# Three of six loads of keys go through ScalarE's DMA queue, in a kernel of windowed attention and two dense blocks

## The chip, the cores and the metric

One NeuronCore of one Trainium2 chip runs the whole kernel. Its engines are TensorE (PE; PEld is its weight load), VectorE (DVE), ScalarE (ACT), GpSimd (POOL) and SyncE (SP). Each has an instruction queue of its own, and they wait for one another through semaphores. The metric is the device time of one execution in microseconds (us), the median of several runs.

## The reference

The attention scores each query against the keys within 16 positions and against 24 block summaries of the keys (the maximum over 32 positions); the values are extended by block means. Its output goes through two dense blocks.

```python
k_sum = k.reshape(B, H, nb, block, D).max(axis=3)      # B, H, S, D = 2, 8, 768, 64; block = 32
v_sum = v.reshape(B, H, nb, block, D).mean(axis=3)
scores_l = scale * np.matmul(q, k.transpose(0, 1, 3, 2))
mask_l = np.abs(pos[:, None] - pos[None, :]) < window  # window = 16
scores_s = scale * np.einsum('bhsd,bhnd->bhsn', q, k_sum) + np.log(block)
...
a = softmax(concatenate([where(mask_l, scores_l, -1e9), scores_s]))
x = matmul(a, concatenate([v, v_sum], axis=2))         # then 1536 tokens x 512
...
h = np.maximum(x @ w_in, 0.0);  x = h * h @ w_out      # first block, 512 -> 2048 -> 512
h = x @ w_in;  g = P(h) / Q(h);  out = g @ w_out       # second block, P and Q polynomials
```

## The kernel before

The kernel runs the attention first, in pieces, and lays the first steps of the dense blocks between them; from about 125 us on, it is the two dense blocks alone: for each of 16 blocks of 128 hidden features and each of three groups of 512 tokens, `l1` (line 630, h) and `l2` (line 724, y) with three matmuls where full precision needs the product of a high and a low part. The weights come as 64-bit words and are decoded on ScalarE, VectorE and GpSimd.

The order of the work of the first part is written out by hand in the string `ORDER`: a list of names that is walked once, and each name calls a function that puts instructions into the queues of its engines. An engine runs its instructions in the order in which they were put there. The names that matter here:

- `E0` to `E5` are `e_load(j)`: load slot j of the keys of the first batch, 128 x 512 floats, 256 KB. Two slots share a buffer: slots 0 and 1 are `early_105`, 2 and 3 `early_106`, 4 and 5 `early_107`. All six go through SyncE's queue (`nc.sync`, line 316), in the order 0, 1, 2, 4, then a load of v (`v1`, line 335), then 3, 5.
- `t0` to `t3` are `k_tr(p)` (line 403): PE transposes the keys of head pair p into two PSUM banks `pk`. t0 reads slots 0 and 1, t1 slots 1 and 2, t2 slots 3 and 4, t3 slots 4 and 5.
- `l0`, `k0`, `l1`, `k1` ... are `k_lin` (line 424): a copy out of one of these banks into `kt`, on ScalarE (on VectorE with a star).
- `q_0`, `q_1`, `Q1` load queries (line 361) through SyncE: four loads of 128 KB, then two of 256 KB.
- `X0`, `X1`, ... are `keep_busy` (line 290): filler matmuls on PE, whose result nobody reads.

The table of ScalarE's functions is loaded by `preload_act_table_set` (line 778), which stands ahead of the walk through the list, so it is ScalarE's first instruction.

Each load reports its landing on one of eight lanes, named DMAHW0 to DMAHW7 in the program. The builder deals the lanes in turn over all queues; a load on a lane that an earlier load had waits, in the queue of the engine that issues it, until that earlier load has landed.

Of the kernel before, what the change touches and what calls it, by code (L numbers as in the profile page):

```python
# [17 lines left out]

ORDER = (
# [32 lines left out]
def tile_window_attention_moe_moe(  # L52
# [13 lines left out]
    nc = tc.nc  # L66
# [111 lines left out]
    T6 = 6  # L178
    NS = 3
    bt = ap.tile([P, WT + (T6 // 2 + 2 * NS) * NB], F32, name="b6", bufs=1)  # L180
    b6 = [bt[:, r * NB:r * NB + HK] for r in range(T6 // 2)]
    b8 = [bt[:, (T6 // 2 + i) * NB:(T6 // 2 + i) * NB + HK] for i in range(2 * NS)]
# [105 lines left out]
    def keep_busy(i):  # L288
# [3 lines left out]
    consts = dict(  # L292
        _i0=c_idle,
        _id=lambda: make_identity(nc, ident), _pr=c_more,
        _m0=lambda: nc.vector.memset(wide, 0.0), _m1=c_window,
        _ml=lambda: nc.vector.memset(mk[:, :, WT:], math.log(BLK) * SC), _m2=c_masks, _b8=c_blocks, _bw=c_blocks6,
    )
# [11 lines left out]
    def flat(src, h, lo, n):  # L309

        x = src[h:h + 4].rearrange("h (p r) d -> (h p) (r d)", r=TR)
        return x[lo * P:(lo + n) * P].rearrange("(s p) x -> p s x", p=P)

    def e_load(j):

        nc.sync.dma_start(
            out=k8[j].rearrange("p (s x) -> p s x", s=1), in_=flat(k[0], j // NS * 4, j % NS, 1)
        )

# [285 lines left out]
    N0 = [0, 5, NF, NF + 9]  # L605
# [167 lines left out]
    G1 = len(tok1) * FS[0] - LEAD[0]  # L773
    dve, act = nc.vector.tensor_copy, nc.scalar.copy
    some, rest = slice(0, 4), slice(4, NWIN)
    v0 = [early[4 + p][:, 0:2 * T6 * D].rearrange("p (h r d) -> p h r d", r=T6, d=D) for p in range(NP)]

    nc.scalar.preload_act_table_set("natural_log_exp_and_others")
    nc.gpsimd.memset(abc[:, 4:5], (1.0 + 1e-6) * 2.0 ** -62)
    nc.gpsimd.memset(abc[:, 5:6], -62.0 * math.log(2.0))  # L780

    def w_next(j, *a):
# [4 lines left out]
    vec = lambda c: nc.vector if c else nc.gpsimd  # L787
    parts = dict(
        E=e_load, v=lambda p: s_load(0, 2 * p, v0[p]), Q=q_load,
        N=lambda i: v_load(i // 4, i % 4 // 2, i % 2), J=k_load,  # L790
        Z=z_load, I=lambda i: w_next(3),
# [12 lines left out]
    G2 = len(tok1) * FS[0] + len(tok2) * FS[1]  # L804
# [122 lines left out]
```

## Time and profile before

| | us |
|---|---|
| median of 3 runs | 601.13 (600.59 to 602.09) |
| profiled execution | 601.2 |
| its span, first to last instruction | 599.5 |

Engines, over the span: PE 592.1 us busy, ACT 392.1, DVE 384.0, POOL 311.6. The chain of work that ended last lies to 93% on PE. The share of PE is so high that the interesting part is the little that is missing from it: nearly all of it lies in the first 100 us. A chain of waits is read backward from the last instruction: each step names what released the next one, a load by "DMA", an engine's queue by a "q" behind its name.

### The profile page before, as it was taken

The page shows a single profiled execution, that of the slowest core. Times are in us where ns is not written, and L with a number is a line of the kernel's source. Part 1 is how long each engine was busy: PE and PEld are TensorE (multiplying, and loading weights), DVE is VectorE, ACT ScalarE, POOL GpSimd, SP SyncE. Part 2 cuts the span into 40 slices and gives each one's busy share as a digit, 9 for nine tenths or more (in the row PEclk, how much of TensorE's full clock was granted, in tenths as well). Part 3 has the DMA queues.
Part 4 walks back from the last instruction along what each step waited for, and adds up shares of the span by engine and source line. Part 5 has one row for each costly group of instructions (what it writes and reads, how often), then busy time and mean ns, then how long its engine had stood idle before and what let it go on. Part 6 is the DMA issues. An engine that isn't in the chain of part 4 may idle for free.

```text
span 599.5 us, 9779 instructions
## 1 busy us (share of the span) xinstructions
PE 592.1 (99%) x3560; PEld 493.6 (82%) x3560; DVE 384.0 (64%) x801; ACT 392.1 (65%) x704; POOL 311.6 (52%) x316
## 2 busy tenths in 40 slices
PE   8999999999999999999999999999999999999997
PEld 8988788888888888888888888888888888888885
DVE  5999977666723331112374778998777876686765
ACT  4999777555644442222565789988888887777772
POOL 1776545412554462222776488676655665445542
PEclk9999999999999999999999999999999999999999
DMA  8989974344532220000254103121211200010101
GB/s 231 248 170 238 243 163 125 102 141 141 175 107 84 93 69 1 0 1 0 71 174 143 35 1 105 36 72 36 71 35 36 71 2 0 1 70 2 47 25 70
DMA packets 64576, 51.49 MB, mean 86 GB/s; under 512 B 39824, under 2 KB 57488, under 8 KB 64528
## 3 DMA queue, kind: packets, MB, share of 16 engines
q1 hardware_dynamic: 64384, 50.74, 30.5%
q8 instruction: 28, 0.46, 0.3%
q14 instruction: 20, 0.16, 0.1%
q10 hardware_dynamic: 144, 0.13, 0.1%
HBM read 47.71 MB, written 3.15 MB: 85 GB/s over the span
## 4 chain that ended last, share of the span: by engine, by line
PE 93%; DVE 3%; DMA 2%; ACT 1%; SPq 0%; issue 0%; DVEq 0%; ACTq 0%
PE h L630 44%; PE y L724 42%; PE pav L577 2%; PE pss L507 2%; PE ptp L557 1%; DMA early<-in_k_dram 1%; PE pt L485 1%; DMA early<-in_v_dram 1%; PE pk L403 1%; PE spare L290 1%; PE pvs L450 0%; DVE pr L523 0%; PE pk L412 0%; DVE acc L756 0%; DVE mx L540 0%; DVE wl L167 0%
## 5 line engine op out<-in xcount | busy, mean ns | idle before, releaser
L630 PE MATMUL h<-xh,wh 128*128 128x512 f32 x384 | 150.6, 392 | 0.0
L630 PE MATMUL h<-xh,wl 128*128 128x512 f32 x384 | 149.5, 389 | 0.0
L630 PE MATMUL h<-xl,wh 128*128 128x512 f32 x384 | 149.5, 389 | 0.0
L654 POOL TENSOR_TENSOR q<-q,u 128x512 f32<-128x512 f32 x48 | 65.2, 1358 | 96.3 <-ACT q L651 91.6
L700 POOL TENSOR_TENSOR sl<-r,sh 128x512 fp32r<-128x512 f32 x42 | 55.0, 1310 | 97.6 <-PE y L724 80.5
L645 DVE TENSOR_TENSOR r<-r,h 128x512 f32<-128x512 f32 x48 | 32.9, 686 | 111.7 <-ACT r L640 104.1
L167 POOL TENSOR_TENSOR wl<-wdec,wh 128x512 fp32r<-128x512 f32 x52 | 69.1, 1334 | 49.6 <-ACT wh L162 35.9
L630 PEld LDWEIGHTS h<-xh,wl 128*128 128x128 f32 x384 | 72.0, 188 | 15.1
L630 PEld LDWEIGHTS h<-xh,wh 128*128 128x128 f32 x384 | 72.1, 188 | 14.7
L630 PEld LDWEIGHTS h<-xl,wh 128*128 128x128 f32 x384 | 72.1, 188 | 14.5
L724 PE MATMUL y<-sh,wh 128*128 128x512 f32 x192 | 75.3, 392 | 0.0
L724 PE MATMUL y<-wh,sl 128*128 128x512 f32 x192 | 74.8, 390 | 0.1
L724 PE MATMUL y<-sl,wh 128*128 128x512 f32 x192 | 74.8, 390 | 0.0
L724 PE MATMUL y<-sh,wl 128*128 128x512 f32 x192 | 74.7, 389 | 0.0
L724 PE MATMUL y<-wh,sh 128*128 128x512 f32 x192 | 74.7, 389 | 0.0
L724 PE MATMUL y<-wl,sh 128*128 128x512 f32 x192 | 74.7, 389 | 0.0
L640 ACT ACTIVATE r<-h 128x512 f32<-128x512 f32 x48 | 28.6, 596 | 66.7 <-PE y L724 35.0
L700 POOL TENSOR_TENSOR sl<-p,sh 128x512 fp32r<-128x512 f32 x48 | 63.1, 1315 | 8.5 <-ACT sh L693 7.1
L676 DVE SCALAR_TENSOR_TENSOR q<-q,h 128x512 f32<-128x512 f32 x48 | 32.9, 686 | 41.6 <-ACT h L672 41.6
L162 ACT CAST wh<-wdec 128x512 fp32r<-128x512 f32 x64 | 39.6, 621 | 27.3 <-DVE wdec L151 27.3
L151 DVE SCALAR_TENSOR_TENSOR wdec<-wraw,wdec 128x512 int32<-128x512 int32 x64 | 49.8, 778 | 2.2
L142 ACT ACTIVATE wdec<-wraw 128x512 f32<-128x512 f32 x64 | 42.3, 666 | 10.6 <-POOL wl L167 6.0
(92 smaller groups left out, 1021.3 us busy)
## 6 DMA issues: line engine op xcount, KB each, us to landing
wraw<-in_moe_w_in_dram SPq DMA_DIRECT2D x32, 512.0 KB, 3.8
wraw<-in_moe_w_out_dram SPq DMA_DIRECT2D x32, 512.0 KB, 3.4
early<-in_v_dram SPq DMA_DIRECT2D x40, 96.0 KB, 4.2
out_dram<-acc SPq DMA_DIRECT2D x11, 256.0 KB, 2.1
acc<-in_q_dram SPq DMA_DIRECT2D x10, 256.0 KB, 6.2
early<-in_k_dram SPq DMA_DIRECT2D x6, 256.0 KB, 5.0
early<-in_v_dram SPq DMA_DIRECT2D x4, 384.0 KB, 5.5
kst<-in_k_dram SPq DMA_DIRECT2D x8, 192.0 KB, 5.4
```

Of the source, the lines that this page charges most:

```text
L142: nc.scalar.activation(out=f32(t), in_=f32(r[:, :, 1]), func=AF.Prelu, scale=2.0 ** -112, alpha=-(2.0 ** 32))
L151: nc.vector.scalar_tensor_tensor(out=t, in0=low, scalar=29, in1=t, op0=ALU.logical_shift_right, op1=ALU.bitwise_or)
L162: copy(out=wt[n][0][:, j], in_=f32(wdec[n, j]))
L167: eng.tensor_tensor(out=tl[:, j], in0=t, in1=f32(th[:, j]), op=ALU.subtract)
L507: nc.tensor.matmul(psc[u][e][w * LO:(w + 1) * LO, c * HK:(c + 1) * HK], lhsT=qz[u % 2][r, c * P + w * LO:c * P + (w + 1) * LO], rhs=kt[2 * ...
L630: nc.tensor.matmul(hq[g][:, 0:n], lhsT=w[:, 0, ws], rhs=x[:, part, ts], start=(part == 0 and j == 0), stop=(part == KC - 1 and j == 2),)
L640: nc.scalar.activation(out=r, in_=hq[g][:, 0:n], func=AF.Relu)
L645: nc.vector.tensor_tensor(out=eq[g], in0=eq[g], in1=hq.pop(g)[:, 0:n], op=ALU.mult)
L654: nc.gpsimd.tensor_tensor(out=q_, in0=q_, in1=u_, op=ALU.mult)
L676: nc.vector.scalar_tensor_tensor(out=q_, in0=q_, scalar=1.0 + 1e-6, in1=z_, op0=ALU.add, op1=ALU.mult)
L700: eng.tensor_tensor(out=sl[:, 0:n], in0=eq.pop(g), in1=f32(sh[:, 0:n]), op=ALU.subtract)
L724: nc.tensor.matmul(o, lhsT=lt, rhs=rt, start=(f == 0 and j == 0 and d * m % 512 == 0), stop=(f == FS[ps] - 1 and j == 2 and (d + 1) * m % ...
```

## The change

`e_load` issues slots 1, 3 and 4 through ScalarE's queue (`nc.scalar`) and slots 0, 2 and 5 through SyncE's. The preload of the table of functions leaves its place ahead of the list and becomes an entry of it, `_pl`, right behind `E3`. Otherwise the list holds the same names in the same order (its lines are broken elsewhere).

```diff
 ORDER = (
     "K1 _i0 _m0 E0 K2 X31 X32 X33 X34 X35 X0 X1 E1 K0 _id t0 k0* l0 c0 B0* E2 _ml _m1 E4 _m2 t1 "
-    "_pr v1 K3 E3 t2 k1 l2 k2 l1* c1 E5 t3 l3 q_0 k3 B1* c2 q_1 q0 z0 X2 c3 S1 q1 z1 B3 X3 s0 s1 "
+    "_pr v1 K3 E3 _pl t2 k1 l2 k2 l1* c1 E5 t3 l3 q_0 k3 B1* c2 q_1 q0 z0 X2 c3 S1 q1 z1 B3 X3 "
...
         _id=lambda: make_identity(nc, ident), _pr=c_more,
+        _pl=lambda: nc.scalar.preload_act_table_set("natural_log_exp_and_others"),
...
     def e_load(j):
 
-        nc.sync.dma_start(
+        dma = nc.scalar if j in (1, 3, 4) else nc.sync
+        dma.dma_start(
             out=k8[j].rearrange("p (s x) -> p s x", s=1), in_=flat(k[0], j // NS * 4, j % NS, 1)
         )
...
-    nc.scalar.preload_act_table_set("natural_log_exp_and_others")
     nc.gpsimd.memset(abc[:, 4:5], (1.0 + 1e-6) * 2.0 ** -62)
```

ScalarE's queue at the program's start, before (kt0 to kt3 are the four pairs of keys, pk the PSUM banks of the transposes):

```order
L922 UNCONDITIONAL_BRANCH [waits barrier_Pool_Activation_PE_DVE_SP_release]
L778 ACT_TABLE_LOAD
L424 COPY kt0_98<-pk_143 128x12x12x4 [waits DVE_49,PE_49]
L424 COPY kt1_99<-pk_124 128x12x12x4 [waits PE_49]
L424 COPY kt2_100<-pk_131 128x12x12x4 [waits PE_49]
L424 COPY kt2_100<-pk_132 128x12x12x4 [waits PE_49]
```

The same place in the change:

```order
L923 UNCONDITIONAL_BRANCH [waits barrier_Pool_Activation_PE_DVE_SP_release]
L318 DMA early_105<-in_k_dram 128x512
L426 ACT_TABLE_LOAD [waits DVE_49]
L426 COPY kt0_98<-pk_142 128x12x12x4 [waits PE_49]
L318 DMA early_107<-in_k_dram 128x512 [waits DMAHW5_49]
L318 DMA early_106<-in_k_dram 128x512 [waits DMAHW7_49]
L295 ACT_TABLE_LOAD
L426 COPY kt1_99<-pk_123 128x12x12x4 [waits PE_49]
```

Slot 1 stands first; slots 4 (`early_107`) and 3 (`early_106`) stand behind the first copy, each with a wait for a lane; a table load stands ahead of that copy and another behind slot 3.

SyncE's queue at the program's start, before (acc is the buffer of the queries):

```order
L316 DMA early_105<-in_k_dram 128x512 x2
L316 DMA early_106<-in_k_dram 128x512
L316 DMA early_107<-in_k_dram 128x512
L335 DMA early_110<-in_v_dram 128x2x384
L316 DMA early_106<-in_k_dram 128x512
L316 DMA early_107<-in_k_dram 128x512
L361 DMA acc_80<-in_q_dram 128x4x64
L361 DMA acc_80<-in_q_dram 128x4x64 [waits DMAHW0_49]
L361 DMA acc_80<-in_q_dram 128x4x64 [waits DMAHW1_49]
```

The same place in the change:

```order
L318 DMA early_105<-in_k_dram 128x512
L318 DMA early_106<-in_k_dram 128x512
L337 DMA early_110<-in_v_dram 128x2x384
L318 DMA early_107<-in_k_dram 128x512
L363 DMA acc_80<-in_q_dram 128x4x64 x3
L363 DMA acc_80<-in_q_dram 128x4x64 [waits DMAHW0_49]
L363 DMA acc_80<-in_q_dram 128x8x64 [waits DMAHW1_49]
L363 DMA acc_80<-in_q_dram 128x8x64 [waits DMAHW2_49]
L129 DMA wraw_395<-in_moe_w_in_dram 128x4x256 [waits DMAHW3_49]
```

SyncE's first eight loads were four slots, v, two slots and one q; its first seven that wait for no lane are now two slots, v, one slot and three q. The order of PE's instructions is the same in both; t2's first matmul waits for lane 7 in the change (lane 5 before).

## Rows read from the trace of the kernel before

**Rows 1.** The page, part 1: busy time, share of the span, instructions

```profile
PE 592.1 (99%) x3560; PEld 493.6 (82%) x3560; DVE 384.0 (64%) x801; ACT 392.1 (65%) x704; POOL 311.6 (52%) x316
```

**Rows 2.** Busy time by stage: stretch, length, PE, PEld, DVE, ACT, POOL, clock, DMA

```profile
0.00:100.00 100.00, 96.64 (x1292) 84.17 (x1294) 82.02 (x332) 78.72 (x192) 57.24 (x116) 1.00 0.89 206
...
200.00:300.00 100.00, 100.00 (x442) 82.79 (x442) 23.64 (x39) 32.55 (x56) 39.17 (x31) 1.00 0.09 29
```

**Rows 3.** The waits of PE: us in total, times, longest

```profile
PE spare L290 <- DVE pp L285: 1.2, 1, 1.2
PE pav L577 <- DMA early<-in_v_dram: 0.8, 1, 0.8
PE pk L403 <- DMA early<-in_k_dram: 0.6, 1, 0.6
PE ptp L557 <- DVE mx L523: 0.6, 1, 0.6
```

**Rows 4.** The chain of waits from the start: start us, us, what

```profile
1.71 0.43 SPq L316
...
2.18 0.43 SPq L316
...
2.65 0.43 SPq L335
...
3.13 5.96 DMA early<-in_k_dram
...
9.14 3.86 PE pk L403 x77
```

**Rows 5.** DMA issues, us to landing: slots 0, 1, 2, 4, v, third q

```profile
early<-in_k_dram SPq DMA_DIRECT2D x1, 256.0 KB, 2.7
...
early<-in_k_dram SPq DMA_DIRECT2D x1, 256.0 KB, 2.9
...
early<-in_k_dram SPq DMA_DIRECT2D x1, 256.0 KB, 4.7
...
early<-in_k_dram SPq DMA_DIRECT2D x1, 256.0 KB, 5.2
...
early<-in_v_dram SPq DMA_DIRECT2D x1, 384.0 KB, 5.7
...
acc<-in_q_dram SPq DMA_DIRECT2D x1, 128.0 KB, 5.6
```

**Rows 6.** Timeline of SyncE's queue, the third load of q: start us, us

```profile
5.72 0.61 SPq L361 DMA_DIRECT2D acc<-in_q_dram  x1
```

**Rows 7.** Timeline of ScalarE from the start: start us, us, what

```profile
0.80 1.28 ACT L778 ACT_TABLE_LOAD   x1 [0.80 <-PEq L909]
5.70 0.64 ACT L424 COPY kt<-pk 128x576 f32<-128x576 f32 x1 [3.62 <-PE pk L403]
```

**Rows 8.** Timeline of PE: fillers, t0 with t1, t2 with t3, later fillers

```profile
1.23 3.36 PE L290 MATMUL spare<-pp 120*128 120x128 f32 x14 [1.23 <-DVE pp L285]
4.51 4.01 PE L403 MATMUL pk<-ident,early 128*64 128x96 f32 x96
9.14 3.86 PE L403 MATMUL pk<-ident,early 128*64 128x96 f32 x96 [0.61 <-DMA early<-in_k_dram]
...
16.20 2.50 PE L290 MATMUL spare<-pp 120*128 120x128 f32 x20
```

**Rows 9.** Stretches at the end; the clock is the number behind POOL's

```profile
597.00:598.00 1.00, 0.00 (x0) 0.00 (x0) 0.00 (x0) 0.00 (x0) 0.00 (x0) 1.00 1.00 347
...
598.60:599.40 0.80, 0.00 (x0) 0.00 (x0) 0.00 (x0) 0.00 (x0) 0.00 (x0) 0.50 0.00 0
```

**Rows 10.** Timeline of PE at the end: its last matmul

```profile
595.29 0.39 PE L724 MATMUL y<-wh,sl 128*128 128x512 f32 x1
```

42 rows, old and new, of the table ORDER are left out of this document.

## Prediction

> **What bounds the kernel now.** I read the page's engine list first [rows 1]: TensorE (PE) is busy 592.1 of 599.5 us, the next engine 392.1. Then the table by stage [rows 2]: in the first 100 us PE is busy 96.64, from 200 to 300 us 100.00. So nothing that happens after the first stage can be hidden by slack on PE, because there is none; and what PE loses in the first stage is added to the end one for one, unless one of its few waits there shrinks by as much. All of PE's idle time with a known releaser is four waits [rows 3]: 1.2 us at the start, 0.6 us before the transposes of keys (pk L403), 0.8 us for v, 0.6 us for VectorE. The program's order on PE is fixed, and the filler matmuls (spare L290) are instructions of that order like all others: a late PE runs them all, so they absorb no delay.
>
> The change touches the second of these waits. The chain of waits [rows 4] shows it: SyncE issues the loads of the key slots one after another, 0.47 us apart; slot 3 is issued at 3.13 us, lands 5.96 us later, and PE starts the transposes t2 at 9.14 us. PE had run out of work at 8.52 us (4.51 + 4.01 [rows 8]).
>
> **What the change removes.** Three issues leave SyncE's queue, so all that stands behind them there moves up by up to 3 x 0.47 = 1.4 us. If all three went out at once on ScalarE, slot 3 would be issued near 1.7 us instead of 3.13. What could that give? The landings say that the transfers, not the issues, set the pace: slot 4 lands at 2.18 + 5.2 = 7.4, v at 2.65 + 5.7 = 8.35, slot 3 at 9.09 [rows 4, 5], 0.7 to 1.0 us apart though issued 0.47 apart. And PE could win no more than the 0.6 us of its wait, as its work lasts to 8.52 us. The Trainium skill says the same (DMA: Bandwidth & Descriptors, section Issuing engines are not separate DMA queues): loads issued on several engines share the same 16 DMA engines, and only the sequencer's issue time is saved. By that rule alone the sum would be 0 to -0.6 us; by the order of instructions below it is not that small.
>
> **What the change moves, and into what.** ScalarE's queue is in order, and the list of work puts l0, the copy of the first transposed keys, ahead of slots 4 and 3. In the order of ScalarE's instructions after the change, slot 1 goes out first; then a table load and the first copy kt<-pk, which waits for PE; then slot 4, which waits for lane 5; then slot 3, which waits for lane 7; then a second table load. So two of the three loads are not issued at the start at all. The copy ran at 5.70 us and took 0.64 [rows 7]: slot 3 cannot be issued before about 6.3 + 0.4 = 6.7 us, against 3.13 before.
>
> The lanes cost more. Lanes are dealt by the time at which the builder expects a load to go out: slots 1, 0, 2 have lanes 0, 1, 2, v 3, slot 5 lane 4, and SyncE's next three loads, of q, take 5, 6 and 7 (they are the three that wait for nothing, and the fourth q waits for lane 0). So slot 4 waits until the first q has landed, slot 3 until the third q has. When is that? Before, the third q was issued at 5.72 us and landed 5.6 us later, at 11.3 [rows 5, 6]. Behind the change slots 4 and 3 are no longer ahead of it. Their shares are what their landings add: slot 4 (2.18 + 5.2) - (1.71 + 4.7) = 0.97 us, slot 3 9.09 - 8.35 = 0.74. That leaves 11.3 - 1.7 = 9.6 us. Bounds: 7.0 us, if q moves up by its issue time (5.72 - 1.4 = 4.3) and then flies as quickly as slot 0 (2.7); 11.3, if nothing is gained.
>
> From 9.6 us slot 3 needs its own flight. The trace shows 2.7 us for slot 0 on empty engines, 2.9 for slot 1 with one load ahead, and 5.96 for slot 3 itself behind five others in one ring. It now has a ring of its own with only slot 4 just ahead, so I take 3.0, near slot 1's 2.9; the ends are 2.7 and 6.0. With 0.1 us for the issue that lies between, slot 3 lands, and t2 starts, at **12.7 us** instead of 9.14: **+3.6 us**. On the bounds it is 9.7 to 17.3, so +0.6 to +8.2.
>
> **What else is moved.** (a) The table load, 1.28 us [rows 7], is now two, since the first copy comes ahead of the preload. The first runs behind slot 1's issue and is over near 2.6 us, three before PE has anything to copy; the second and the copy of t1 (0.64 us) start when slot 3 is issued and end 1.9 us later, under slot 3's flight of 2.7 or more. Zero; with that cover gone it would be 1.28. (b) Slots 0 and 1 start together, not 0.45 us apart. t0 needs both, but waits behind 14 fillers until 4.5 us [rows 8]; zero, within 0.3 either way. (c) Slot 2 moves up by one issue; t1 starts near 6.5 us, about its landing at 1.71 + 4.7 = 6.4; zero to -0.2. (d) v, slot 5 and q land earlier. Nobody on the path waits for them there.
>
> **The clock.** PE now has nothing to do from 8.52 to about 12.7 us, 4.2 us; before, its longest stop was 1.2 us. Two places tell what such a stop does. At the end the last matmul ends at 595.7 us [rows 10]; the granted clock is still 1.00 at 597 to 598 us and 0.50, the level of 1.2 GHz, at 598.6 [rows 9]: it had fallen within 2.9 us of idling. At the start, the 14 fillers take 3.36 us, 0.24 each, while 20 of the same kind take 2.50 later, 0.125 each [rows 8]: PE ran at half speed for its first 3.3 us of work. So a stop of 4.2 us, if it does what the end shows, costs half of 3.3 us behind it: **+1.6 us**; 0 if the clock holds, 3.3 if it stays low twice as long.
>
> **What is late next.** Everything of the attention hangs on t2 and t3 through PE, so ScalarE, VectorE and GpSimd move along with it. The two waits left, 0.8 us for v and 0.6 for VectorE [rows 3], could shrink, as weights and later loads that don't depend on PE come relatively earlier. The v load is itself issued after a PE step; I take **-0.4 us**, bounds 0 and -1.4.
>
> Sum on the profiled execution: 601.2 + 3.6 + 1.6 - 0.4 = 606.0 us. That execution is 0.07 above the median of the three runs (601.13), so against the median 605.9.
>
> **The rivals.**
> *The same wait, but the clock holds.* The stop is 4.2 us, not much more than the 2.9 us after which it had fallen at the end, and one fall is thin evidence. Time: 601.13 + 3.6 - 0.4 = 604.3.
> *Not slower: the lanes are free early.* The place is slot 3's issue on ScalarE. If the third q lands near the lower bound of 7.0 us, slot 3 goes out then and lands near 9.9: +0.7 us and no stop long enough for the clock, 601.8. The point from which it decides: with a flight of 3.0, the result leaves the band of no change only if slot 3 is issued after about 8.3 us. For it: the engines carry 768 KB less ahead of that q in SyncE's ring. Against it: 512 KB of that is merely unsent, and all landings before show 0.7 to 1.0 us for each 256 KB.
> *The loads do go out first*, as the words of the change have it: if ScalarE issued all three ahead of its copies, slot 3 would land by about 8.4 and PE's 0.6 us would go: 600.5. The order of instructions speaks against it flatly.
> *Slot 3 stands behind SyncE's traffic.* If its flight is 6.0 us as before, with q and the first weights ahead of it, t2 starts at 15.7: +6.6 + 1.6 - 0.4, 608.9. The Trainium skill (DMA: Bandwidth & Descriptors, section Queues, rings and completion order) says that each DMA engine takes turns between the rings that have work, a packet at a time, which speaks against a full 6.0. No row here shows two loaded rings at once; by that rule the flight is nearer the short end, and the sum the likeliest one above.
>
> **How the numbers follow.** Likeliest, wait and fallen clock, 605.9: 0.50, with a range of its own of 603.9 to 608.2 from a landing one to two us off. Wait alone, 604.3: 0.27. Slot 3 behind the traffic, 608.9: 0.10. Lanes free early, 601.8: 0.08. Loads first, 600.5: 0.03. The rest, 0.02, I leave to what I don't see, half of it faster. The range of 602.6 to 608.8 leaves out the two small cases below and most of the one above. About 0.3%, 1.8 us, is what a measurement of this kernel can tell from no change, so slower begins at 602.9. The first three cases, less a tail of the second, give slower 0.85; the two at 601.8 and 600.5 and that tail give same 0.13; faster 0.02, since PE's whole idle time at this spot is 0.6 us.
>
> **What would show it.** In the profile after: slot 1 issued on ScalarE near 0.8 us, but slots 4 and 3 only after the first copy, each at the moment the first and third q land, near 8.7 and 9.6; two table loads; PE idle before the second group of pk transposes for about 4 us, released by the load of k; fillers or transposes behind it at half speed and a granted clock under 1.00 near 11 to 16 us; after 100 us the same PE work as before, shifted. I am wrong if slot 3 is issued before 8.3 us, if the second group starts before 11 us, or if a later wait of PE takes the delay back.

## The result, and the profile after

The changed kernel takes 610.73 us (median of 4 runs, 607.68 to 611.14), the kernel before 601.61 in the same comparison (600.59 to 602.14): 1.0143 times as long, 95% interval 1.0106 to 1.0179. It is slower, as forecast, but by 9.1 us between the medians where 4.8 were forecast, and above the range. The profiled execution took 610.62 us, its span 608.9 against 599.5 before: +9.4 us. These 9.4 us are what has to be found.

The page's first part and the stages come first, as in [rows 1, 2]; columns are stretch, length, PE, PEld, DVE, ACT, POOL, clock, share of the DMA engines, GB/s:

```profile
PE 595.4 (98%) x3560; PEld 496.8 (82%) x3560; DVE 383.4 (63%) x801; ACT 393.4 (65%) x705; POOL 312.1 (51%) x316
```

```profile
12.00:16.00 4.00, 0.00 (x0) 0.00 (x0) 1.33 (x3) 0.27 (x1) 0.00 (x0) 0.78 1.12 291
16.00:20.00 4.00, 3.38 (x50) 3.38 (x51) 0.00 (x0) 0.64 (x1) 0.00 (x0) 0.50 0.47 117
...
0.00:100.00 100.00, 90.66 (x1190) 79.63 (x1190) 74.18 (x305) 72.80 (x176) 50.47 (x102) 0.97 0.82 196
200.00:300.00 100.00, 100.00 (x443) 82.84 (x442) 22.77 (x38) 31.48 (x55) 37.94 (x30) 1.00 0.08 27
```

PE does nothing at all from 12 to 16 us, and works at the lower of its two clock levels (0.50, 1.2 GHz) from 16 to 20. The stage from 200 to 300 us is full, as before: the loss lies at the start and is never made up.

The waits of PE, to be held against [rows 3] (us in total, times, longest):

```profile
PE pk L405 <- DMA early<-in_k_dram: 6.9, 1, 6.9
PE spare L290 <- DVE pp L285: 1.2, 1, 1.2
PE ptp L559 <- DVE mx L525: 0.6, 1, 0.6
PE pav L579 <- DMA early<-in_v_dram: 0.6, 1, 0.6
```

The four waits are the same four. Together they grew from 3.2 to 9.3 us, by 6.1. PE's busy time grew by 3.3 (592.1 to 595.4): together the 9.4. The timeline of PE, as in [rows 8], shows the two halves (start us, us, what, idle before and releaser):

```profile
1.23 3.36 PE L290 MATMUL spare<-pp 120*128 120x128 f32 x14 [1.23 <-DVE pp L285]
4.52 5.17 PE L405 MATMUL pk<-ident,early 128*64 128x96 f32 x96
16.62 5.86 PE L405 MATMUL pk<-ident,early 128*64 128x96 f32 x96 [6.94 <-DMA early<-in_k_dram]
22.41 0.66 PE L487 MATMUL pt<-ident,acc 128*128 128x128 f32 x4
```

t2 starts at 16.62 us, not at 9.14: +7.48. t2 and t3 take 5.86 us, not 3.86, and the transposes of q behind them start at 22.41, not at 12.93: +9.48, so +2.0 for the lower clock. Nearly the whole difference of the spans is there by 22.4 us; all that comes later gives back 0.1. (t0 and t1 took 5.17 instead of 4.01. PE's rate rose later in this run: 34 of its matmuls run from 5 to 7 us, as many as from 8 to 9 alone, where the kernel before has 32 from 5 to 6. The clock column reads 1.00 there in both kernels, but the trace's first entry for the clock stands at 7.44 us, and at 4.55 before. The delay lies under the wait for slot 3 and costs nothing.)

Why t2 is late stands in the chain of waits, as in [rows 4], and in ScalarE's timeline, as in [rows 7]:

```profile
3.74 6.21 DMA acc<-in_q_dram
...
9.97 6.61 DMA early<-in_k_dram
...
16.62 5.86 PE pk L405 x80
```

```profile
0.80 0.41 ACTq L318 DMA_DIRECT2D early<-in_k_dram  x1
1.48 1.28 ACT L426 ACT_TABLE_LOAD   x1 [1.48 <-DVE pk L393]
6.53 0.64 ACT L426 COPY kt<-pk 128x576 f32<-128x576 f32 x1 [3.77 <-PE pk L405]
8.88 1.43 ACTq L318 DMA_DIRECT2D early<-in_k_dram  x2
10.34 1.28 ACT L295 ACT_TABLE_LOAD   x1 [3.17 <-DMA acc<-in_q_dram]
```

Slot 1 goes out at 0.80 us. Then comes the copy at 6.53; behind it slot 4 goes out at 8.88, when the first load of q lands (8.86), and slot 3 at 9.97, when the third has (9.95). The order of steps is the predicted one, instruction by instruction. What was not predicted is the 6.61 us that slot 3 takes from there.

### The profile page after: what moved, and what is told of

Read it like the earlier page. It is cut to its first block, busy times and chain, and to the rows that moved or that the text cites. A ratio compares the mean times of both kernels' runs of the same rounds, so it can differ in the third digit from the quotient of the medians.

```text
span 608.9 us, 9778 instructions
## 1 busy us (share of the span) xinstructions
PE 595.4 (98%) x3560; PEld 496.8 (82%) x3560; DVE 383.4 (63%) x801; ACT 393.4 (65%) x705; POOL 312.1 (51%) x316
## 4 chain that ended last, share of the span: by engine, by line
PE 92%; DMA 3%; DVE 3%; ACT 1%; SPq 1%; issue 0%; DVEq 0%; ACTq 0%
PE h L632 43%; PE y L726 41%; PE pav L579 2%; PE pss L509 2%; PE ptp L559 1%; DMA early<-in_k_dram 1%; DMA acc<-in_q_dram 1%; PE pk L405 1%; PE pt L487 1%; DMA early<-in_v_dram 1%; PE spare L290 1%; PE pvs L452 0%; DVE pr L525 0%; PE pk L414 0%; DVE acc L758 0%; DVE mx L542 0%
```

## The experiments

All are the changed kernel with one thing altered, if nothing else is said. "Flight" is the time from a load's issue to its landing. Numbers from a single profiled run are given as such.

### Slots 3 and 4 alone, slot 1 alone

```diff
-        dma = nc.scalar if j in (1, 3, 4) else nc.sync
+        dma = nc.scalar if j in (3, 4) else nc.sync      # e4_slots34
+        dma = nc.scalar if j in (1,) else nc.sync        # e3_slot1
```

> The changed kernel with slot 1 back on SyncE's queue; slots 4 and 3 alone go through ScalarE's. Theory A: both still stand behind the copy and wait for the lanes of q, which is about 0.4 us later with one more issue on SyncE; slot 3 issued near 10.2, PE's stop 6 to 8 us, 610 to 612 us. Rival D: a gain of over 2 us against the changed kernel, below 608.5 us.

> The changed kernel with slot 1 alone on ScalarE's queue; slots 3 and 4 back on SyncE's; the preload stays where the change put it, so there are still two table loads. Theory A: as before, slot 3 issued at 2.7 instead of 3.1 us, landing 8.6 to 9.1, 601 to 602 us; the second table load costs nothing. Rival D (the move of slot 1 or the extra table load costs by itself): 602.9 us or more.

With slots 3 and 4 alone on ScalarE the time is 610.01 us, ratio 1.0148 (1.0125 to 1.0172); with slot 1 alone 601.60, ratio 1.0004 (0.9995 to 1.0014). The loss is all in slots 3 and 4. First the chain and the PE timeline of slots 3 and 4 alone, then the PE timeline of slot 1 alone:

```profile
4.20 5.73 DMA acc<-in_q_dram
...
9.95 5.87 DMA early<-in_k_dram
```

```profile
15.86 6.04 PE L405 MATMUL pk<-ident,early 128*64 128x96 f32 x96 [6.35 <-DMA early<-in_k_dram]
```

```profile
4.51 8.01 PE L405 MATMUL pk<-ident,early 128*64 128x96 f32 x192
```

In the last, t0 to t3 are one unbroken group: slot 3, issued on SyncE at 2.66 us, lands at 8.51, early enough. That kernel also loads ScalarE's table twice, at 1.47 and 6.84 us, so the second table load costs nothing where it has cover.

### The loads ahead of ScalarE's other work

```diff
-    "K1 _i0 _m0 E0 K2 X31 X32 X33 X34 X35 X0 X1 E1 K0 _id t0 k0* l0 c0 B0* E2 _ml _m1 E4 _m2 t1 "
-    "_pr v1 K3 E3 _pl t2 k1 l2 k2 l1* c1 E5 t3 l3 q_0 k3 B1* c2 q_1 q0 z0 X2 c3 S1 q1 z1 B3 X3 "
+    "K1 _i0 _m0 E0 K2 X31 X32 X33 X34 X35 X0 X1 E1 E4 E3 _pl K0 _id t0 k0* l0 c0 B0* E2 _ml _m1 _m2 t1 "
+    "_pr v1 K3 t2 k1 l2 k2 l1* c1 E5 t3 l3 q_0 k3 B1* c2 q_1 q0 z0 X2 c3 S1 q1 z1 B3 X3 "
```

> The changed kernel with slots 4 and 3 and the table load put right behind slot 1 in the list, ahead of the first copy; nothing waits for a lane there. Theory A (the loss comes from where slots 4 and 3 stand in ScalarE's queue: behind a copy and behind the lanes of two loads of q): all three go out by 1.8 us, slot 3 lands at 8.4 to 9.1 us, PE's stop before t2 is 0 to 0.6 us, the time is that of before, 601 to 602 us. Rival B (ScalarE's DMA queue is slow of itself, or two loaded queues slow each other): flights on ScalarE's queue more than 1 us longer than those of SyncE's loads issued beside them, t0 or t2 late by that, 603 us or more.

The same three loads on the same queue, but ahead of the copy that waits for PE: 601.64 us, ratio 1.0002 (0.9993 to 1.0012). So neither ScalarE's queue nor the three loads on it cost anything that can be measured; where they stand in it does. The first row of ScalarE's timeline (the three issues), and PE's timeline:

```profile
0.80 1.38 ACTq L318 DMA_DIRECT2D early<-in_k_dram  x3
```

```profile
4.51 7.92 PE L405 MATMUL pk<-ident,early 128*64 128x96 f32 x192
12.36 0.66 PE L487 MATMUL pt<-ident,acc 128*128 128x128 f32 x4
...
40.18 1.04 PE L579 MATMUL pav<-pp,early 120*64 120x64 f32 x28 [1.19 <-DMA early<-in_v_dram]
...
58.08 1.35 PE L579 MATMUL pav<-pp,early 120*64 120x64 f32 x32 [0.33 <-DMA early<-in_v_dram]
```

Slot 3 lands at 7.89 us (8.4 to 9.1 was expected), PE's wait for it is gone, and the transposes of q start 0.57 us earlier (12.36 against 12.93). That was the whole prize, and it doesn't reach the end: the matmul that waits for v waits 1.19 us instead of 0.77 and starts at 40.18 instead of 40.33, so 0.15 is left, and a second wait for v of 0.33 us appears at 58 us.

### One table load

```diff
-    "K1 _i0 _m0 E0 K2 X31 X32 X33 X34 X35 X0 X1 E1 K0 _id t0 k0* l0 c0 B0* E2 _ml _m1 E4 _m2 t1 "
-    "_pr v1 K3 E3 _pl t2 k1 l2 k2 l1* c1 E5 t3 l3 q_0 k3 B1* c2 q_1 q0 z0 X2 c3 S1 q1 z1 B3 X3 "
+    "K1 _i0 _m0 E0 K2 X31 X32 X33 X34 X35 X0 X1 E1 _pl K0 _id t0 k0* l0 c0 B0* E2 _ml _m1 E4 _m2 t1 "
+    "_pr v1 K3 E3 t2 k1 l2 k2 l1* c1 E5 t3 l3 q_0 k3 B1* c2 q_1 q0 z0 X2 c3 S1 q1 z1 B3 X3 "
```

> The changed kernel with the preload of the functions right behind slot 1, ahead of the first copy, so that there is one table load again; slots 4 and 3 stand and wait as in the change. Theory A: the second table load cost nothing, PE's stop stays 6 to 7 us, 609 to 611.5 us. Rival E (the second table load, right behind slot 3, holds something on the path): 1.3 us less or more, below 609 us in the median, with a stop shorter by 1 us or more.

With the preload right behind slot 1 there is one table load: 609.36 us, ratio 1.0143 (1.012 to 1.0165), the ratio with two. The intervals leave room for the 1.3 us of rival E, and in the profiled run PE's stop is 5.42 us, 1.5 shorter than with two, as that rival had it. But with two the second table load starts at 10.34 us, when slot 3 is already issued, and the copy behind it ends at 12.27, 4.3 us before slot 3 lands; nothing on the path waits for it. The shorter stop comes from slot 3, which went out at 9.61 us, at the third q's landing again, and had a shorter flight. Chain of waits:

```profile
3.73 5.86 DMA acc<-in_q_dram
...
9.61 4.50 DMA early<-in_k_dram
```

Slot 3's flight, begun each time at the third q's landing, was thus 6.61, 5.87 and 4.50 us in three profiles, and 5.41 in that of the next run. It is never near 3.0. That the shortest belongs to the one kernel with a single table load isn't explained.

### The clock alone

```diff
-    "_pr v1 K3 E3 _pl t2 k1 l2 k2 l1* c1 E5 t3 l3 q_0 k3 B1* c2 q_1 q0 z0 X2 c3 S1 q1 z1 B3 X3 "
+    "_pr v1 K3 E3 _pl "
+    "X36 X37 X38 X39 X40 X41 X42 X43 X44 X45 X46 X47 X48 X49 X50 X51 X52 X53 X54 X55 X56 X57 X58 X59 X60 X61 X62 X63 X64 X65 t2 k1 l2 k2 l1* c1 E5 t3 l3 q_0 k3 B1* c2 q_1 q0 z0 X2 c3 S1 q1 z1 B3 X3 "
```

> The changed kernel with 30 more filler matmuls (6.7 us at the full clock) between t1 and t2, where PE stands idle for 6.9 us. Theory A: slot 3 still lands near 16.6 us, but the clock doesn't fall, and t2 with t3 take 3.9 us instead of 5.9: 2.0 us less, 608.7 us. Rival C (t2 and t3 are slow for another reason, such as the transfers beside them): still 5.9 us, 610.7 us.

Thirty filler steps (60 matmuls) keep PE busy while slot 3 is under way. They cost their own time only where they run past its landing; the time is 608.63 us (608.45 to 610.41), ratio 1.0133 (1.0117 to 1.0149). PE's timeline, and the granted clock by stretch:

```profile
9.23 6.96 PE L291 MATMUL spare<-pp 120*128 120x128 f32 x60
16.13 3.86 PE L406 MATMUL pk<-ident,early 128*64 128x96 f32 x96
```

```profile
12.00:16.00 4.00, 4.00 (x38) 4.00 (x36) 1.33 (x3) 0.36 (x1) 0.00 (x0) 1.00 1.03 263
16.00:20.00 4.00, 4.00 (x99) 3.81 (x99) 1.04 (x2) 1.92 (x3) 0.00 (x0) 1.00 0.63 134
```

With PE kept at work the clock holds at 1.00, and t2 and t3 take 3.86 us again, though t2 starts at 16.13: the 2.0 us of the changed kernel are the clock's. In this run slot 3 landed at 15.09, not near 16.6 as expected, so the fillers themselves delayed t2 by 1.0 us; of the 2.0 that they save, 1.0 is left. That the time still meets theory A's 608.7 is luck, and by the times alone this kernel can't be told from the changed one (1.0117 to 1.0149 against 1.0106 to 1.0179): the rows show the clock's part.

### What the flight waits for: less traffic behind slot 3

```diff
-    "_pr v1 K3 E3 _pl t2 k1 l2 k2 l1* c1 E5 t3 l3 q_0 k3 B1* c2 q_1 q0 z0 X2 c3 S1 q1 z1 B3 X3 "
+    "_pr v1 K3 E3 _pl t2 k1 l2 k2 l1* c1 _hq E5 t3 l3 q_0 k3 B1* c2 q_1 q0 z0 X2 c3 S1 q1 z1 B3 X3 "
+        _hq=lambda: nc.vector.memset(qr[1][:, :, :, 0:1], 0.0),
...
+    def c_hold():
+        r = hp.tile([P, DM, 2], I32, tag="stage", name="wraw", bufs=3)
+        nc.vector.memset(r[:, 0:1, 0], 0)
+        held_w.append(r)
```

> The changed kernel, but SyncE's two loads of 256 KB of q, and all behind them, the first weights too, wait for a small memset that VectorE does after the summaries of the second pair of keys, near 12 us. The builder then deals lanes 1 and 2 to slots 4 and 3, whose earlier loads landed long ago, so both go out right behind the first copy, near 7.2 and 7.6 us, with only four small loads of q in flight. Theory F (slot 3's flight of 6.6 us in the change was long because SyncE's loads lay ahead of it in the shared engines): a flight of 2.7 to 3.7 us, t2 starts at 10.5 to 11.5. Rival G (a load on ScalarE's queue is slow so late, whatever lies beside it): a flight of 4.6 us or more, t2 after 12.2. The time, with SyncE's later loads held back, 603 to 608 us.

> As the run before, but only the first load of weights and what stands behind it on SyncE waits for the memset; the two loads of 256 KB of q go out as in the change. The lanes are 3 and 4, free when v and slot 5 have landed, so slot 4 is issued near 7.5 and slot 3 near 8.3 us. Theory F: a flight between the two, 4 to 5.3 us, t2 at 12.3 to 13.6. Rival G: 6 us or more, t2 after 14.3. The time 604 to 609 us.

A small write of VectorE into a load's destination holds that load, and with it all that SyncE has behind it, until later. In the first kernel (`_hq`, behind `c1`) the two loads `Q1` are held, in the second (`c_hold`, at the same place) the first weights, w_in. As the deal of lanes changes with that, slots 4 and 3 also get other lanes: free ones in the first kernel, those of v and slot 5 in the second. The first gave 604.9 us, the second 607.48, one run each (before, beside them: 601.01, median of 13). ScalarE, chain of waits, and the DMA queues from 6 to 8 us and from 8 to 12 us (packets, MB, share of 16 engines; q1 is SyncE's queue, q10 ScalarE's), all of the first:

```profile
5.71 0.82 ACTq L319 DMA_DIRECT2D early<-in_k_dram  x2
```

```profile
6.09 5.72 DMA early<-in_k_dram
...
11.85 4.16 PE pk L406 x57
```

```profile
q1 hardware_dynamic: 1434, 0.62, 113.7%
...
q10 hardware_dynamic: 288, 0.52, 41.5%
q1 hardware_dynamic: 866, 0.21, 30.7%
```

This is where my first explanation fell. With nothing of SyncE's behind slot 3 I expected a short flight; it was 5.72 us, outside theory F's range and inside rival G's. The loads went out earlier than expected, though, with v, slot 5 and the four small loads of q not landed yet. Slots 4 and 3, issued at 5.71 and 6.09, had not moved one packet by 8 us (no row of q10 from 6 to 8), while 1434 packets of SyncE's queue ran; slot 4's and slot 3's packets came from 8.26 us on, and they landed at 11.17 and 11.81, right behind the fourth load of q (10.50), which in the changed kernel, with no key load beside it, landed at 10.51. So in this run the two loads waited for the traffic ahead, although it was on the other queue. It is not always so: the first packet of slot 4 ran 2.55 us after its issue here, but 1.49 after it in the changed kernel and 1.09 in the second kernel, both times with loads of SyncE's not landed. In the second kernel slot 3, issued at 7.81, took 5.48, between the ranges of F and G. These two runs don't exclude G; the next two test it.

### Another queue, and empty engines

```diff
-    "K1 _i0 _m0 E0 K2 X31 X32 X33 X34 X35 X0 X1 E1 K0 _id t0 k0* l0 c0 B0* E2 _ml _m1 E4 _m2 t1 "
-    "_pr v1 K3 E3 _pl t2 k1 l2 k2 l1* c1 E5 t3 l3 q_0 k3 B1* c2 q_1 q0 z0 X2 c3 S1 q1 z1 B3 X3 "
+    "K1 _i0 _m0 E0 K2 X31 X32 X33 X34 X35 X0 X1 E1 K0 _id t0 k0* l0 c0 B0* E2 _ml _m1 _m2 t1 "
+    "_pr v1 K3 _pl E5 q_0 q_1 E4 E3 t2 k1 l2 k2 l1* c1 _hq t3 l3 k3 B1* c2 q0 z0 X2 c3 S1 q1 z1 B3 X3 "
-        dma = nc.scalar if j in (1, 3, 4) else nc.sync
+        dma = nc.scalar if j in (1,) else nc.sync
...
-    "_pr v1 K3 E3 _pl t2 k1 l2 k2 l1* c1 E5 t3 l3 q_0 k3 B1* c2 q_1 q0 z0 X2 c3 S1 q1 z1 B3 X3 "
+    "_pr v1 K3 E3 _pl t2 k1 l2 k2 l1* c1 _hp _hq E5 t3 l3 q_0 k3 B1* c2 q_1 q0 z0 X2 c3 S1 q1 z1 B3 X3 "
+        _hq=lambda: nc.vector.memset(qr[1][:, :, :, 0:1], 0.0), _hp=lambda: nc.vector.memset(qr[0][:, :, :, 0:1], 0.0),
```

> As the run with SyncE's two loads of 256 KB held by a memset, but slots 4 and 3 are issued by SyncE, right behind the four small loads of q, near 5.1 and 5.6 us; slot 1 stays on ScalarE's queue. Theory H (the shared engines serve loads in the order in which they are issued, whichever queue they come from): they land right behind the fourth q, near 11.2 and 11.8 us, within 0.5 of where they landed through ScalarE's queue (11.17 and 11.81), t2 near 11.9, the time within 1.5 us of 604.9. Rival G (ScalarE's queue is slow by itself): slot 3 lands at least 1 us earlier than there, at 10.8 us or before.

> As the run with the two loads of 256 KB of q held, but the four small ones are held by the same memset too, so that only slots 0, 1, 2, 5 and v lie ahead when slots 4 and 3 go out through ScalarE's queue, right behind the first copy near 5.7 and 6.1 us. Theory H: they land right behind slot 5 (7.9 to 8.3 us), slot 4 at 8.6 to 9.0 and slot 3 at 9.2 to 9.7, a flight of 3.1 to 3.7 us, t2 at 9.3 to 9.8 and the clock doesn't fall there. Rival G: a flight of 4.6 us or more as in all runs so far, slot 3 after 10.7. The time hangs on the held loads of q, which PE needs 3.9 us behind t2: 601.5 to 606 us.

The first of the two (upper diff) leaves only slot 1 on ScalarE and puts slots 4 and 3 behind the same four loads of q on SyncE's queue, with Q1 held as above: 605.77 us (one run; before beside it 600.69). The chain, PE, and the granted clock (0.70) from 12 to 16 us:

```profile
4.82 2.62 SPq L319
...
7.49 4.78 DMA early<-in_k_dram
```

```profile
12.31 5.40 PE L406 MATMUL pk<-ident,early 128*64 128x96 f32 x96 [2.91 <-DMA early<-in_k_dram]
```

```profile
12.00:16.00 4.00, 3.69 (x71) 3.69 (x72) 1.39 (x5) 1.28 (x2) 0.00 (x0) 0.70 0.51 117
```

Slot 3 is issued at 7.49 us, not near 5.6, as slot 4's issue took 2.62, and lands at 12.27; through ScalarE, issued 1.4 us earlier, it had landed at 11.81. Slot 4 lands at 10.62 here and had landed at 11.17. So the two queues differ by half a microsecond, once either way, and rival G, which had slot 3 land 1 us earlier here, is out. Behind a stop of only 2.91 us the clock fell here too: it is 1.00 from 12 to 13 us and 0.50 from 14 to 17, and t2 and t3 take 5.40 us instead of 3.86.

The second (lower diff) keeps slots 4 and 3 on ScalarE and holds the loads of q as well, so that only slots 0, 1, 2, 5 and v are ahead. Its DMA issues on ScalarE (slot 4; the second one is in the next sentence) and PE:

```profile
early<-in_k_dram ACTq DMA_DIRECT2D x1, 256.0 KB, 2.8
```

```profile
10.00 3.86 PE L406 MATMUL pk<-ident,early 128*64 128x96 f32 x96 [0.35 <-DMA early<-in_k_dram]
15.60 0.30 PE L488 MATMUL pt<-ident,acc 128*128 128x128 f32 x1 [1.73 <-DVE kss L435]
```

Slots 4 and 3 went out at 6.53 and 6.90 us, the last load ahead of them (slot 5) landed at 7.24, and they took 2.8 and 3.06 us, their first packet 1.3 us after the issue. That is the flight I had predicted, on the same queue: it is the price of empty engines. The time, 606.43 us (one run; 601.5 to 606 was expected), is no gain, because the held queries are now late: the first of them lands at 15.46, where PE would need it at 13.87. The wait of 1.73 us is put down to VectorE's kss, which ended at 15.54, a little behind that landing; waits of 0.64 and 0.44 us for q itself follow.

### v behind the keys, on the kernel before

```diff
-    "_pr v1 K3 E3 t2 k1 l2 k2 l1* c1 E5 t3 l3 q_0 k3 B1* c2 q_1 q0 z0 X2 c3 S1 q1 z1 B3 X3 s0 s1 "
+    "_pr K3 E3 t2 k1 l2 k2 l1* c1 E5 v1 t3 l3 q_0 k3 B1* c2 q_1 q0 z0 X2 c3 S1 q1 z1 B3 X3 s0 s1 "
```

> The kernel before, all loads on SyncE, but with the first load of v behind slots 3 and 5. Slot 3 lands near 8.3 us, ahead of PE's need, and t2 starts without a stop, 0.6 us earlier. If what the loads could give at this place reaches the end: 601.0 us, 0.6 less than before. If a later wait takes it back, as it did with all three loads first on ScalarE (there PE was 0.57 us ahead at 28 us, and behind after 58 us): 601.3 to 602, no change.

If landings follow the order of issue, the kernel before should lose its 0.6 us of waiting by having slot 3 issued ahead of v. It takes 601.56 us, ratio 1.0009 (1.0 to 1.0018). PE's timeline:

```profile
4.45 5.64 PE L403 MATMUL pk<-ident,early 128*64 128x96 f32 x144
10.72 2.08 PE L403 MATMUL pk<-ident,early 128*64 128x96 f32 x48 [0.62 <-DVE pk L391]
...
40.65 1.03 PE L577 MATMUL pav<-pp,early 120*64 120x64 f32 x28 [1.29 <-DMA early<-in_v_dram]
```

The theory holds, slot 3 lands at 7.38 us and t2 doesn't wait; but t3 now waits 0.62 us for VectorE to prepare a PSUM bank (line 391, a memset of pk), and the wait for v grows from 0.77 to 1.29. No kernel of this study is measurably faster than the one before.

## Why the prediction was right or wrong

**What bounds the kernel: right.** PE's loss at the start went to the end one for one: 9.48 us late at 22.41, 9.4 at the end. (Of the 7.4 us that PE is not busy in the kernel before, 3.4 lie in the first 100 us and 3.8 behind its last matmul, so "nearly all" of it in the first 100 us was too much.)

**The order on ScalarE and the lanes: right.** Slots 4 and 3 waited for the first copy, then for the landings of the first and third q. Slot 3's issue was predicted for 9.7 us and came at 9.97: 0.3 of the miss. The order of instructions, not the words of the change, told this; the same loads ahead of the copy cost nothing.

**The flight of slot 3: the step that failed.** The term was 3.0 us with bounds of 2.7 and 6.0; it measured 6.61, beyond the upper bound, and 4.50 to 6.61 in the profiles in which it went out at the third q's landing. It makes 3.6 of the 4.6 us by which the profiled execution exceeds the sum of 606.0. I took the value from slot 1, which flew with one load ahead of it, because slot 3 would have "a ring of its own". But at 9.97 us four loads of SyncE's were on the engines beside slot 4, all issued before it: the fourth q (landed 10.51), the two halves of Q1 (12.51 and 14.16) and the first w_in (17.22). The nearest row was the one I put at the other end, slot 3's own 5.96 us behind five loads. Moving a load later doesn't move it out of the traffic when SyncE goes on issuing: the space that the key loads left was filled by Q1 and the weights.

The packets of the trace, taken in order of their start, split the flight. Slot 4's first packet ran 1.49 us after its issue, against 1.33 on empty engines (the run with all of q held), so standing in line added little in the changed kernel. But the packets of slots 4 and 3 took 4.96 us (10.37 to 15.33) beside SyncE's, against 1.75 on empty engines. And from slot 3's last packet to its landing it took 1.25 us, against 0.34: a load signals its landing in sixteen parts, and of slot 3's twelve were there by 14.64, the fifteenth at 15.54, the last at 16.58.

By the Trainium skill (DMA: Bandwidth & Descriptors, section Queues, rings and completion order) each DMA engine takes turns between the rings that have work; I used this to argue for the short flight. The traces agree in part. Where both queues have packets, they do run side by side, though no view shows the turns of a single engine; the DMA queues of the changed kernel from 13 to 15 us:

```profile
q1 hardware_dynamic: 853, 0.46, 79.2%
q10 hardware_dynamic: 125, 0.23, 30.7%
```

There ScalarE's queue moves 0.23 MB beside SyncE's 0.46, and slot 4, issued 0.86 us after the second half of Q1, landed 0.63 us ahead of it. But running side by side did not shorten a flight to that of empty engines, and with Q1 held ScalarE's queue moved nothing for 2.55 us after the issue, where 1.33 is what it takes on empty engines. Sharing the engines cost slot 3 as much as standing in line. The Trainium skill's rule that loads of all issuing engines run on the same 16 DMA engines (the same page, section Issuing engines are not separate DMA queues) was the better guide for this term.

**The clock: right in kind, near in size.** Predicted +1.6 us, bounds 0 and 3.3; measured +2.0. The kernel with fillers shows that it is the clock. The granted clock stays at 0.50 until 21 us (0.50 from 20 to 21, 0.95 from 21 to 22), so about 4.4 us of PE's work ran at the lower level, where 3.3 had been taken.

**What is late next: small, and smaller than taken.** Predicted -0.4 us, measured -0.1: the wait for v shrank from 0.8 to 0.6 us, the one for VectorE stayed at 0.6.

**The table load and slots 0 and 1 together: right at zero, as far as the runs can tell.** With one table load less the ratio is the same 1.0143, within intervals of 0.2 to 0.4%, and slot 1 alone on ScalarE, with both table loads, is at 1.0004.

**The sum, put right.** 606.0 + 0.3 (q's landing) + 3.6 (flight) + 0.4 (clock) + 0.3 (later waits) = 610.6, the profiled execution's own time.

**The rivals and the range.** The right case was the last of the four, slot 3 behind SyncE's traffic, at 608.9 with a chance of 0.10. My reason against it was a rule, with no row of this kernel under it, and I said myself that no row showed two loaded queues. With nothing but a rule for the short end, this case deserved a chance nearer to that of the likeliest, and the range should have reached past its 608.9, since that was taken with the middle of the clock's bounds. The two rivals near zero were excluded on good grounds: slot 3 was issued 1.7 us after the 8.3 us from which the change had to show.

**What stays open.** Why slot 3's flight differs by 2 us among runs in which it goes out behind the same loads. Of the difference between 6.61 and 4.50, 1.5 us lie before its last packet and 0.6 behind it (1.25 and 0.63 us to the landing). In the changed kernel the last three packets of ScalarE's queue start later than 15 us, all others before, and the last landing signals trail; that would fit one or two of the 16 DMA engines lagging, but the trace doesn't name a packet's engine. A fetch of 16 KB of instructions, one packet of 1.28 us from 9.61 to 10.89, falls between slot 3's issue and its first packet, but no run here ties the two together. Open, too, is why ScalarE's queue had to wait for its first packet in one run and not in others. The runs in which loads are held are single ones.

## What to carry to other kernels

A load that is issued by a compute engine stands in that engine's line: before moving it, read which instruction stands ahead of it there, what that one waits for, and which earlier load its own semaphore lane belongs to. Price its flight by what is already on the engines when it goes out, from a row with as much ahead of it, not by how empty its own queue is. And where the engine at the bound stops for some microseconds, add what its clock then costs.

## What the runs showed of the hardware that I had not expected

- A second queue doesn't always give a late load an early turn: issued at 5.71 us on a queue with nothing else in it, slot 4 had its first packet at 8.26, 2.55 us later, against 1.33 on empty engines. In two other kernels with loads of SyncE's under way it took 1.09 and 1.49.
- The same 256 KB (slots 4 and 3, issued late) took 2.8 to 3.1 us on empty engines and 4.1 to 6.6 with other loads on them.
- The last of a load's sixteen landing signals can trail the fifteenth by about 1 us: 16.58 against 15.54 for slot 3 in the change, 9.09 against 8.17 in the kernel before, where PE's wait of 0.6 us hangs on it; with Q1 held it was 11.81 against 11.79.
- An issue itself can take long: slot 4's on SyncE took 2.62 us behind four loads of q, where 0.43 is usual [rows 4].
- The clock fell behind a stop of only 2.91 us (1.00 from 12 to 13 us, 0.50 from 14 to 17), and t2 and t3 behind it took 5.40 us instead of 3.86.
